# A new instruction order for the last two thirds of a fused adaLN, dilated-attention and SwiGLU block

## The chip, the cores and the metric

One core of a Trainium2 chip runs the whole program in one launch. The metric is the device time of one execution in microseconds; a kernel's time is the median of its runs. The profile is one execution recorded by the hardware profiler: its span runs from the first to the last recorded instruction, and its own time is a little longer than the span.

## The reference

A transformer block over 2048 tokens of width 512. A conditioning vector gives six vectors of 512 (shift, scale and gate for each half). The first half is a windowed attention: 32 heads of 16, each token looks at 8 keys, at distances 0, 2, ..., 14. The second half is a SwiGLU feed-forward network (FFN) with 1792 hidden units.

```python
mod = (_silu(c) @ w_mod).reshape(c.shape[0], 6, 1, -1)
sa, ca, ga, sb, cb, gb = ...
h = _layernorm(x) * (1 + ca) + sa
x = x + ga * _A_ref(h, A_wqkv, A_wo)      # window of 8, dilation 2
h = _layernorm(x) * (1 + cb) + sb
x = x + gb * _B_ref(h, B_w1, B_w3, B_w2)  # (silu(h w1) * (h w3)) w2
```

All inputs and the result are bfloat16.

## The kernel before

**How the work is cut.** The tokens are 16 tiles of 128. Attention runs by pairs of tiles; the last four are softmaxed as two pairs with one exponential step. The FFN runs in six blocks of tiles (list `FFN`): block 0 has tiles 0 and 1, block 1 tiles 2 and 3, block 2 tiles 4 to 7, block 3 tiles 8 to 11, block 4 tiles 12 and 13, block 5 tiles 14 and 15. Blocks 2 and 3 so have 512 columns, the others 256. Attention of late tiles runs beside the FFN of early ones.

**The steps of an attention tile T**, with the lines that the profile names:
- L742, VectorE: the product of queries and shifted keys ("product"), 4096 elements a partition.
- L752, TensorE: the scores, 16 small tiled matmuls, written S in the lists below.
- L764, L769 on VectorE: maximum and subtraction; L782 on ScalarE: the exponential, with a table load before it, and another (L889) when the next gate activation follows; L794, L796, L797 on VectorE: sum, reciprocal, normalisation; L807 on TensorE: a turn of the weights (T), copied out by L811 on ScalarE.
- The shifted values are loaded from a scratch tensor in device memory by four DMAs a tile (tiles `sb_vsh`, `sb_vshx`; three buffers in all). L827, VectorE: values times weights ("value product"). L855, TensorE: the sum over the window, 8 tiled matmuls ("value sum", A). L861 on ScalarE copies it to `sb_ac`; a DMA transposes it into `sb_ot`.
- L867, TensorE: the output projection (O), 4 matmuls. L871, VectorE: the residual, which also gives the sum for the mean.

**The second layer norm**, by pairs of tiles: L586 on GpSimd (minus the mean), L590 on ScalarE for each tile (squares and their sum), L596, L597, L599 on GpSimd (variance, power, bias), L601 on ScalarE for each tile (the normalised tile), a DMA transpose for each tile into `sb_h`, and L621 on ScalarE, four times for a block (scale and shift).

**The FFN.** For each of 14 hidden tiles of a block: the gate half (g, L883 with `w1`, 4 matmuls), L889 on ScalarE (silu), the up half (u, L883 with `w3`), L892 on VectorE (product of both). The second layer Z of a tile is 14 matmuls in two halves a and b of 7 (L921); for tiles 14 and 15 it is cut by columns instead, 28 matmuls of 256 columns each (L909). L931 on VectorE adds the residual, and a DMA stores the tile. L952 on VectorE scales `w2` by the gate vector, in four pieces.

**What sets the order.** `_build` records 1118 operations with what they read and write. The list `ORDER` says in which order they are issued, one list for all five engines, so each engine's own order is a part of it; `SLOTS` says which buffer each pooled value gets (8 banks of PSUM, 3 buffers for h, 5 for the normalised tiles, 6 for the silu results, 20 for the hidden tiles and so on). `synchronize` then derives the waits from data dependencies and from the reuse of buffers:

```python
for v in o.vals:
    if v.pool is not None and v.pool.last.get(v.slot) is not v:
        before = v.pool.last.get(v.slot)
        if before is not None:
            o.prev.extend(before.users)
```

Each engine executes its list strictly in that order, and a wait holds everything behind it on that engine. All but one of the DMAs are issued by SyncE (SP), in its own order, and a DMA's issue waits for its source and its target buffer.

Of the kernel before, what the change touches and what calls it, by code (L numbers as in the profile page):

```python
# [272 lines left out]
def _build(p, A_x, A_wqkv, A_wo, B_w1, B_w3, B_w2, c, w_mod, out):  # L273
# [752 lines left out]
]  # L1026
SLOTS = [
# [19 lines left out]
]  # L1047


# [26 lines left out]
```

## Time and profile before

| | us |
|---|---|
| median of 3 runs | 241.81 (240.87 to 242.73) |
| the profiled execution, its own time | 241.33 |
| its span | 239.6 |
| TensorE busy | 231.9 |
| VectorE busy | 179.2 |
| ScalarE busy | 138.8 |
| GpSimd busy | 30.0 |
| mean granted TensorE clock | 1.00 |

A row of the order in time has the start, the length, the engine, the line, the operation, the tiles (output first), and in brackets how long the engine sat idle before it and what released it. "PE" is TensorE's matmuls, "PEld" its weight loads, "SPq" the issuing of DMAs on SyncE. Rows merge equal neighbours, with their number behind an x.

### The profile page before, as it was taken

Reading aid. Unit: us, or ns where it says so; the run is one execution under the profiler, and the core shown is the slowest. Engines: PE = TensorE matmul, PEld = TensorE weight load, DVE = VectorE, ACT = ScalarE, POOL = GpSimd, SP = SyncE. Lnnn points to the kernel's source line nnn. Section 1 sums busy time; section 2 is a strip of 40 time slices with the busy share of each in tenths; the row PEclk is TensorE's granted clock in tenths of the full one; section 3 lists DMA queues with packets and bytes.
Section 4 is the critical chain, followed back from the end, with each engine's and each line's share of the span. In section 5 each row is a group of like instructions: output and inputs, shape, how many; then the busy total and the mean of one; then the engine's idle time right before and its main releaser. Section 6 shows DMA issues by size and latency. Waiting matters only on the chain.

```text
span 239.6 us, 4572 instructions
## 1 busy us (share of the span) xinstructions
PE 231.9 (97%) x1806; PEld 135.9 (57%) x1806; DVE 179.2 (75%) x279; ACT 138.8 (58%) x267; POOL 30.0 (13%) x66
## 2 busy tenths in 40 slices
PE   7899999999999999999999999988999999999995
PEld 4676554545688684664444444433374484566774
DVE  5689999999999999999999989381555125234243
ACT  2289577899978737958735792636466043322210
POOL 4434000013002000420005220032020000000000
PEclk9999999999999999999999999999999999999999
DMA  6999999999999995998953995341300700010102
GB/s 210 373 336 309 138 244 299 214 270 310 335 291 255 250 204 168 248 191 240 228 153 90 198 228 58 96 122 36 77 22 12 100 0 0 3 43 2 47 22 66
DMA packets 46317, 38.85 MB, mean 162 GB/s; under 512 B 21704, under 2 KB 37080, under 8 KB 46296
## 3 DMA queue, kind: packets, MB, share of 16 engines
q1 hardware_dynamic: 46288, 38.56, 67.7%
q8 instruction: 14, 0.23, 0.4%
q14 instruction: 7, 0.06, 0.1%
q10 hardware_dynamic: 8, 0.00, 0.0%
HBM read 29.62 MB, written 4.21 MB: 141 GB/s over the span
## 4 chain that ended last, share of the span: by engine, by line
PE 79%; DMA 6%; DVE 5%; SPq 4%; ACT 2%; POOL 2%; issue 1%; DVEq 0%
PE pall L883 36%; PE pall L921 16%; PE pall L691 7%; PE pall L867 6%; DMA sb_x<-in_A_x_dram 5%; SPq L124 4%; PE pall L711 4%; PE pall L752 3%; PE pall L855 3%; PE pall L909 3%; DVE sb_pq L742 2%; DMA sb_ot<-sb_ac 1%; DVE sb_vsh L827 1%; POOL sb_nm L586 1%; DVE sb_st L555 1%
## 5 line engine op out<-in xcount | busy, mean ns | idle before, releaser
L883 PE MATMUL pall<-sb_h,sb_w 128*128 128x256 bf16 (+1 forms) x672 | 102.9, 308 | 1.7 <-ACT sb_sg L889 1.7
L883 PEld LDWEIGHTS pall<-sb_h,sb_w 128*128 128x128 bf16 x672 | 64.8, 98 | 38.1 <-ACT sb_sg L889 2.1
L892 DVE TENSOR_TENSOR sb_hh<-sb_sg,pall 128x256 bf16<-128x256 bf16 (+1 forms) x84 | 40.0, 506 | 37.8 <-PE pall L883 32.6
L889 ACT ACTIVATE sb_sg<-pall 128x256 bf16<-128x256 f32 (+1 forms) x84 | 35.7, 453 | 50.9 <-PE pall L883 49.0
L921 PE MATMUL pall<-sb_w,sb_hh 128*128 128x512 bf16 x196 | 45.1, 379 | 0.0
L742 DVE TENSOR_TENSOR sb_pq<-sb_q,sb_kT 128x4096 bf16<-128x4096 bf16 x16 | 36.4, 2283 | 0.0
L691 PE MATMUL pall<-sb_h,sb_wqkv 128*128 128x512 bf16 (+1 forms) x160 | 31.1, 336 | 0.4 <-DVE sb_st L555 0.4
L921 PEld LDWEIGHTS pall<-sb_w,sb_hh 128*128 128x128 bf16 x196 | 19.1, 98 | 21.2 <-issue 0.4
L827 DVE TENSOR_TENSOR sb_vsh<-sb_vsh,sb_al 128x4096 bf16<-128x4096 bf16 x12 | 27.3, 2285 | 0.0
L621 ACT ACTIVATE sb_h<-sb_h,sb_modc 128x512 bf16<-128x512 bf16 (+1 forms) x24 | 16.5, 742 | 9.5 <-DMA sb_h<-sb_xn 9.5
L691 PEld LDWEIGHTS pall<-sb_h,sb_wqkv 128*128 128x128 bf16 x160 | 14.6, 97 | 12.1 <-DVE sb_st L555 0.6
L931 DVE TENSOR_TENSOR sb_o<-pall,sb_x 128x512 bf16<-128x512 f32 (+1 forms) x18 | 11.1, 625 | 10.0 <-PE pall L921 6.2
L586 POOL TENSOR_SCALAR sb_nm<-sb_sx 128x2 f32<-128x2 f32 x8 | 3.7, 464 | 108.4 <-DVE sb_x L871 108.3
L867 PE MATMUL pall<-sb_wo,sb_ot 128*128 128x512 bf16 x64 | 15.8, 379 | 0.5 <-DMA sb_ot<-sb_ac 0.5
L711 PE MATMUL pall<-sb_wqkv,sb_h 128*128 128x512 bf16 x64 | 16.0, 379 | 0.0
L871 DVE SCALAR_TENSOR_TENSOR sb_x<-pall,sb_x 128x512 bf16<-128x512 f32 x16 | 10.9, 687 | 4.6 <-PE pall L867 4.2
L644 ACT ACTIVATE sb_h<-pall,sb_modc 128x256 bf16<-128x256 bf16 (+1 forms) x18 | 9.9, 611 | 7.5 <-DVE sb_modc L509 6.5
L590 ACT ACTIVATE sb_xn<-sb_x,sb_nm 128x512 bf16<-128x512 bf16 x16 | 11.4, 716 | 4.8 <-POOL sb_nm L586 4.8
L861 ACT ACTIVATE sb_ac<-pall 128x512 bf16<-128x512 f32 x16 | 9.4, 597 | 7.0 <-PE pall L855 6.8
L601 ACT ACTIVATE sb_xn<-sb_x,sb_nb,sb_rs 128x512 bf16<-128x512 bf16 x16 | 12.2, 804 | 1.5 <-POOL sb_nb L599 1.4
L555 DVE BATCH_NORM_STATS2 sb_st<-sb_x 128x6 f32<-128x512 bf16 x16 | 10.5, 680 | 1.4 <-DMA sb_x<-in_A_x_dram 1.4
L701 ACT ACTIVATE sb_kT<-pall 128x512 bf16<-128x512 f32 x16 | 9.6, 606 | 2.8 <-PE pall L691 2.7
(87 smaller groups left out, 206.7 us busy)
## 6 DMA issues: line engine op xcount, KB each, us to landing
sb_vsh<-v_scratch_dram SPq DMA_DIRECT2D x48, 256.0 KB, 5.4
sb_vshx<-v_scratch_dram SPq DMA_DIRECT2D x16, 256.0 KB, 5.1
sb_w<-in_B_w_dram SPq DMA_DIRECT2D x6, 512.0 KB, 7.2
sb_w<-in_B_w_dram SPq DMA_DIRECT2D x6, 384.0 KB, 4.1
v_scratch_dram<-sb_v SPq DMA_DIRECT2D x16, 128.0 KB, 6.0
out_dram<-sb_o SPq DMA_DIRECT2D x14, 128.0 KB, 1.8
sb_wqkv<-in_A_wqkv_dram SPq DMA_DIRECT2D x6, 256.0 KB, 6.5
sb_x<-in_A_x_dram SPq DMA_DIRECT2D x4, 256.0 KB, 6.5
```

The source lines that it names most:

```text
L555: o = p.op("dve", lambda e, T=T: e.bn_stats(st[:, T, :], x_sb[:, T, :]), 595, ("st", T), r=[vx[T]], w=[vs])
L601: p.op("act", lambda e, vn=vn, T=T: e.activation(vn.at[:], x_sb[:, T, :], ACT.Identity, bias=nb[:, T, :], scale=rs[:, NT + T, :]), c_act(5 ...
L621: return e.activation(vh.at[:, ft, 0:n * P], vh.at[:, ft, 0:n * P], ACT.Identity, bias=modc[:, 8 * which + ft:8 * which + ft + 1], scale=m ...
L691: ins = e.matmul(bank(vp)[:, j * n:(j + 1) * n], wqkv[:, t, col:col + P], vh.at[:, t, 0:n], start=(t == ORDER[0] and j == 0), stop=(t == O ...
L711: ins = e.matmul(bank(vp), vh.at[:, t, tt * P:(tt + 1) * P], wqkv[:, t, 2 * D:3 * D], start=(t == ORDER[0]), stop=(t == ORDER[-1]))
L742: return e.tensor_tensor(vp.at[:], in0, in1, ALU.mult)
L827: return e.tensor_tensor(v_w, v_w, a_w, ALU.mult)
L867: ins = e.matmul(bank(vy), vt.at[:, ft, :], wo[:, ft, :], start=(ft == 0), stop=(ft == KT - 1))
L883: ins = e.matmul(bank(vp)[:, 0:n], wt[:, t, fi * P:(fi + 1) * P], vh.at[:, t, 0:n], start=(t == 0), stop=(t == KT - 1))
L889: p.op("act", lambda e: e.activation(vt.at[:, 0:n], bank(vgp)[:, 0:n], ACT.Silu), c_act(n), k, r=[vgp], w=[vt], table="silu")
L892: p.op("dve", lambda e: e.tensor_tensor(vh_.at[:, 0:n], vt.at[:, 0:n], bank(vup)[:, 0:n], ALU.mult), c_dve(n), k, r=[vt, vup], w=[vh_])
L921: ins = e.matmul(bank(vz), vhh[fi].at[:, tt * P:(tt + 1) * P], w2[:, fi, :], start=(fi == 0), stop=(fi == NF - 1))
```

## The change

`ORDER` and `SLOTS` get new contents; no other line of the file differs. Of the 1118 entries of `ORDER` the first 560 stay; from there on all engines have the same operations in a new order (on TensorE from its 187th operation of 384, on VectorE from the 131st of 263, on ScalarE from the 119th of 241, on GpSimd from the 41st of 62, on SP from the 89th of 168). `SLOTS` changes from its 74th entry on: of the first 560 operations 143 use another PSUM bank, and ten of TensorE's have their waits moved; their order is the same.

```diff
@@ ORDER
-    429, 710, 711, 456, 457, 712, 713, 722, 723, 724, 727, 728, 729, 455, 732, 733, 440, 725, 430, 746, 698, 699, 459, 53, 702, 703,
-    480, 54, 470, 471, 472, 734, 735, 441, 442, 460, 461, 345, 346, 714, 431, 432, 738, 762, 462, 481, 497, 482, 473, 474, 483, 675,
...
+    429, 710, 711, 456, 457, 712, 713, 702, 703, 727, 718, 719, 720, 721, 746, 747, 748, 749, 738, 480, 739, 740, 741, 714, 324,
+    455, 459, 715, 716, 717, 698, 699, 700, 732, 733, 53, 701, 440, 441, 442, 481, 430, 470, 471, 482, 54, 483, 460, 461, 722, 431,
...
@@ SLOTS
-    2, 3, 6, 1, 5, 0, 7, 5, 7, 6, 2, 2, 1, 4, 0, 1, 3, 1, 2, 0, 4, 1, 4, 0, 7, 0, 1, 3, 6, 3, 0, 4, 2, 5, 1, 2, 1, 1, 0, 2, 4, 0, 6,
+    2, 3, 6, 1, 5, 0, 7, 5, 7, 6, 2, 2, 1, 4, 0, 1, 3, 1, 2, 0, 4, 1, 4, 0, 7, 5, 1, 3, 6, 3, 0, 4, 2, 0, 1, 2, 1, 1, 0, 2, 4, 0, 1,
...
```

What the numbers mean, for TensorE from the last common operations to the first of block 4. g1.3 is the gate half of hidden tile 3 in block 1; S, A, O, T are scores, value sum, output projection and turn of a tile, Z4a the first half of tile 4's second layer. Before:

```
g1.3 u1.3 | g1.6 u1.6 u1.7 u1.8 g1.12 g1.0 g1.1 A7 g1.9 O5 A6 g1.4 O4 g1.10 O7 Z0b O6 u1.1 u1.4 u1.0 g1.5 u1.5 Z1b g1.13 u1.9 u1.12 T8 u1.10 u1.13 Z2a Z3a Z3b Z2b A9 S11 S10 A8
g2.3 g2.8 g2.11 u2.11 u2.8 g2.9 g2.7 O9 T10 O8 g2.12 g2.5 g2.0 u2.12 g2.2 g2.13 u2.5 A11 S12 S13 A10 g2.1 u2.2 u2.0 g2.6 g2.4 u2.1 S14 S15 O11 O10 u2.4 u2.6 u2.9 u2.3 g2.10 u2.7 u2.13 T12 u2.10 Z6a Z7a Z4a Z4b A13 A12 Z5a Z6b T14
g3.3 g3.1 O13 O12 g3.5 u3.5 g3.12 g3.4 u3.4 Z5b A15 A14 g3.9 u3.12 Z7b u3.1 g3.2 O14 O15 g4.4 ...
```

After:

```
g1.3 u1.3 | g1.1 g1.5 u1.5 g1.12 u1.12 g1.10 u1.10 g1.4 u1.4 g1.0 u1.0 u1.8 O5 A7 A6 g1.6 O4 g1.9 u1.9 u1.1 u1.7 T8 O7 O6 u1.6 Z1b Z0b g1.13 u1.13 Z2a Z2b Z3a Z3b S11 S10 A9 A8
g2.0 g2.2 u2.0 g2.12 g2.4 g2.10 u2.4 T10 O9 O8 g2.3 u2.3 g2.7 g2.5 g2.1 u2.1 u2.2 g2.11 A11 S13 S12 A10 g2.13 u2.10 u2.5 g2.8 u2.8 O11 g2.6 u2.6 S14 S15 g2.9 O10 u2.7 u2.11 u2.13 u2.12 u2.9 T12 Z5a Z7a Z6a Z6b Z7b A12 A13
g3.2 u3.2 T14 g3.0 Z4a g3.8 O12 u3.0 O13 g3.6 g3.9 Z4b g3.5 u3.5 g3.1 u3.8 A14 A15 g3.3 g3.12 u3.3 u3.6 g3.4 u3.4 Z5b g4.5 ...
```

Behind that, blocks 3 and 4 and the second layer of tiles 8 to 11 are mixed, then block 5 and the second layer of 12 to 15, in both orders; O14 and O15 come after 9 and 19 operations of that mixture in the new one.

On the other engines, as far as the text below speaks of them:
- VectorE, after value product 6: before, the residuals of 5, 4, 7 and 6 among two pieces of `w2`'s scaling (between 5 and 4) and the first sum of Z; after, residual 5, three softmax steps of tiles 8 and 9 around residual 4, both pieces of the scaling, residuals 7 and 6, one L892, the product for tile 11, three L892, the product for tile 10, value products 9 and 8, then four sums of Z mixed with L764 and L769 of tiles 10 and 11 (before: two sums there).
- VectorE around the end of attention: before, residuals 13 and 12 directly followed by value products 15 and 14; after, value product 15, residual 12, a sum of Z, an L892, residual 13, a sum of Z, value product 14.
- ScalarE: before, the L590 of tiles 13 and 12 stand ahead of the silu of three gate halves of block 3 that had been computed; after, they stand behind the silu of five.
- SP: before, all loads of the values of tile 9 are issued ahead of the transposes for tiles 4 to 7; after, its fourth load stands behind the first of these transposes. The write of tile 13's values to the scratch tensor goes ahead by some 25 us, the transposes of the value sums 5 and 4 stand between the two loads of `w2`.

78 rows, old and new, of tables (ORDER, SLOTS) are left out of this document.

## The prediction

> **What bounds the kernel now.** I read the page first, then the busy time by stretches of 10 us, then the chain that ended last, then TensorE (PE) alone in order of time, and last all engines around its gaps.
>
> ```profile
> span 239.6 us, 4572 instructions
> PE 231.9 (97%) x1806; PEld 135.9 (57%) x1806; DVE 179.2 (75%) x279; ACT 138.8 (58%) x267; POOL 30.0 (13%) x66
> ```
>
> ```profile
> 120.00:130.00 10.00, 10.00 (x87) 4.65 (x86) 10.00 (x11) 5.49 (x12) 2.07 (x2) 1.00 0.45 114
> ```
>
> PE is busy in 97% of the span (a stretch's first number is its length, the next PE, then weight loads, VectorE, ScalarE, GpSimd). Between 30 and 143 us VectorE (DVE) is as full as PE; this row is one of that stretch. So no order can win much: it can only close gaps on PE. A PE row's length holds its pipeline; what one operation occupies is read from the chain, where pieces follow without a gap.
>
> ```profile
> 118.17 0.86 PE pall L867 x4
> 119.04 0.22 PE pall L807 x4
> 120.12 6.04 PE pall L883 x28
> ...
> 225.96 2.62 PE pall L883 x24
> 228.58 1.51 PE pall L921 x7
> ...
> 230.97 6.13 PE pall L909 x56
> ```
>
> A wide matmul thus takes 0.216 us (6.04/28), so an FFN half of 4 (gate or up) 0.86 at 512 columns; 2.62/24 = 0.109, so 0.44 at 256 columns; half a second-layer tile 1.51; an output projection 0.86; a turn of the softmax 0.22. Now PE's starts, and what stands between them:
>
> ```profile
> 110.10 0.61 PE L855 MATMUL pall<-sb_vshx,sb_ind 128*32 128x512 bf16 x8
> ...
> 111.42 0.61 PE L855 MATMUL pall<-sb_vsh,sb_ind 128*32 128x512 bf16 x8
> 111.96 6.22 PE L883 MATMUL pall<-sb_h,sb_w 128*128 128x512 bf16 x28
> ...
> 149.24 1.05 PE L855 MATMUL pall<-sb_vsh,sb_ind 128*32 128x512 bf16 x16
> 150.22 3.19 PE L921 MATMUL pall<-sb_w,sb_hh 128*128 128x512 bf16 x14
> ```
>
> ```profile
> 156.93 3.62 PE L883 MATMUL pall<-sb_h,sb_w 128*128 128x512 bf16 x16
> ...
> 157.75 2.29 DVE L827 TENSOR_TENSOR sb_vshx<-sb_vshx,sb_al 128x4096 bf16<-128x4096 bf16 x1
> 157.92 2.19 POOL L586 TENSOR_SCALAR sb_nm<-sb_sx 128x2 f32<-128x2 f32 x1 [16.87 <-DVE sb_x L871]
> ...
> 160.14 0.72 ACT L590 ACTIVATE sb_xn<-sb_x,sb_nm 128x512 bf16<-128x512 bf16 x1 [4.14 <-POOL sb_nm L586]
> ...
> 161.57 1.06 ACT L889 ACTIVATE sb_sg<-pall 128x512 bf16<-128x512 f32 x2
> ...
> 162.20 1.04 PE L883 MATMUL pall<-sb_h,sb_w 128*128 128x512 bf16 x4 [1.66 <-ACT sb_sg L889]
> ...
> 166.16 1.90 PE L883 MATMUL pall<-sb_h,sb_w 128*128 128x512 bf16 x8
> ...
> 169.41 1.89 PE L883 MATMUL pall<-sb_h,sb_w 128*128 128x512 bf16 x8
> ...
> 171.81 1.90 PE L867 MATMUL pall<-sb_wo,sb_ot 128*128 128x512 bf16 x8 [0.51 <-DMA sb_ot<-sb_ac]
> ```
>
> Three gaps. (a) The 16 matmuls of 156.93 end at 160.39, the next start at 162.20: 1.81. (b) From 162.20 come 4 + 7 matmuls and the value sums of tiles 15 and 14 (0.98 for two, 149.24 to 150.22): 165.56, but the next start is 166.16: 0.60. (c) 169.41 + 1.73 = 171.14, next 171.81: 0.67, for the transposed value sum. Together 3.08 us, all in the stretch in which FFN block 3 runs beside the last attention tiles. From 112 to 153 PE has none, and from 173.5 to the last matmul (230.97 + 6.13) there is 0.2.
>
> Why (a): row 157.92 is the mean of tiles 12 and 13 on GpSimd (POOL). It begins 0.17 after a value product on DVE and takes 2.19 where the same operation takes 0.22 (row 95.83 below): it comes out 0.07 after the product. Behind it on ScalarE (ACT) stand two L590, and behind those the gate activation (161.57) that frees the bank PE wants.
>
> **The change, part by part.** Everything up to PE's 86.95 us (86.08 and two halves of 0.44) keeps its order; some PSUM banks there are renumbered, which moves ten PE waits to a neighbour. I count nothing for it. The last stage, from the first matmul of 230.97 to the end (239.6 - 230.97 = 8.63), has the same instructions and the same kind of tail, so also nothing. Three legs are left, in each of which I add PE's work in the new order and ask which chain is later.
>
> ```profile
> 94.90 0.58 ACT L782 ACTIVATE pall<-pall 128x512 f32<-128x512 f32 x1
> 95.50 1.28 ACT L889 ACT_TABLE_LOAD   x1
> 95.83 0.22 POOL L586 TENSOR_SCALAR sb_nm<-sb_sx 128x2 f32<-128x2 f32 x1 [18.51 <-DVE sb_x L871]
> 97.07 0.71 ACT L590 ACTIVATE sb_xn<-sb_x,sb_nm 128x512 bf16<-128x512 bf16 x1
> ...
> 98.66 0.19 POOL L596 TENSOR_SCALAR sb_rs<-sb_var 128x2 f32<-128x2 f32 x1 [2.62 <-ACT sb_xn L590]
> 99.10 0.70 POOL L597 TENSOR_TENSOR sb_rs<-sb_rs,sb_cst 128x2 f32<-128x2 f32 x1
> 99.88 0.19 POOL L599 TENSOR_TENSOR sb_nb<-sb_nm,sb_rs 128x2 f32<-128x2 f32 x1
> 99.94 2.28 DVE L742 TENSOR_TENSOR sb_pq<-sb_q,sb_kT 128x4096 bf16<-128x4096 bf16 x1
> ...
> 101.13 1.51 ACT L601 ACTIVATE sb_xn<-sb_x,sb_nb,sb_rs 128x512 bf16<-128x512 bf16 x2
> 101.96 5.15 SPq L124 DMA_TRANSPOSE sb_h<-sb_xn  x4
> 103.29 0.60 ACT L811 ACTIVATE sb_al<-pall 128x512 bf16<-128x512 bf16 x1 [0.38 <-PE pall L807]
> 106.27 0.41 DVE L892 TENSOR_TENSOR sb_hh<-sb_sg,pall 128x256 bf16<-128x256 bf16 x1
> 106.60 2.29 DVE L827 TENSOR_TENSOR sb_vshx<-sb_vshx,sb_al 128x4096 bf16<-128x4096 bf16 x1
> 108.62 2.93 ACT L621 ACTIVATE sb_h<-sb_h,sb_modc 128x512 bf16<-128x512 bf16 x4 [3.33 <-DMA sb_h<-sb_xn]
> 111.64 0.69 DVE L764 TENSOR_REDUCE sb_mx<-pall 128x64 f32<-128x512 f32 x1
> 111.95 0.11 PEld L883 LDWEIGHTS pall<-sb_h,sb_w 128*128 128x128 bf16 x2 [0.42 <-ACT sb_h L621]
> ```
>
> *Leg 1, to the first half of block 2 (111.96 before).* Up to there PE has 20 halves of 0.44 (8.7), 4 projections (3.4), 2 value sums together (1.1), a turn (0.2), 6 second-layer halves (9.1) and two scores with two value sums (111.96 - 110.10 = 1.9): 24.4, ready at 111.35, against 111.96. But row 111.95 shows that PE waited there for L621, the last link of the layer norm of tiles 4 to 7, and this is what counts. The chain begins with projection 6, the last of the four. In the new order PE reaches it at 86.95 + 11.3 = 98.3, its end (99.15) and DVE's residuals of 7 and 6 (behind the two w2 scalings) put residual 6 at 99.68. POOL starts 0.78 after a residual starts (95.05 to 95.83 in the row's stage): 100.46. ACT is busy with L601 of tile 4 and a gate until 101.3, then two L590 of 0.71; 0.88 after the second starts (98.66 stands so to the L590 behind 97.07) L596, then L597 and L599 (98.66 to 100.07), done near 104.1. Two L601 (1.51) end at 105.6; two transposes at 1.25 on SP (row 101.96: four in 5.15) end at 107.5, against 107.11. L621 begins 1.5 after that (108.62 - 107.11) and PE 3.34 after L621 begins: 112.35. That is 0.4 later than before, though PE would have been 0.6 earlier.
>
> *Leg 2, to the first half of block 3.* PE: 28 wide halves 24.2, scores and value sums 1.9 + 1.0 + 1.0, 4 projections 3.4, 2 turns 0.4, now 5 second-layer halves ahead of it, 7.6: 39.4, ready at 151.8. The chain: the scores of tiles 14 and 15 come after 22 halves, 3 projections, a turn and 1.9, and take 0.9, so at 136.95; DVE's L764 and L769 (0.69 each as 111.64) 138.3; two exponentials (0.58 each), the table (1.28) and gate 9 (0.5) on ACT 141.2; two L590, POOL's three, L601, L811, L601 as above (1.5 + 1.25 + 2.1) 146.1; one transpose 147.35; to PE 1.5 + 3.34 again: 152.2. DVE must deliver value product 12 by 150.8: its operations there are those of before with one more of 0.6, and its span then, 111.00 to 149.5, holds 0.6 idle, so it ends near 149.9. That cover of 0.9 is the narrowest in this leg.
>
> *Leg 3, to 230.97 before.* Here the new order has 17 of block 3's halves ahead of block 4 where the old one had 11, and projections 14 and 15 go behind block 4's first halves: 17 x 0.86 + 2 projections 1.7 + 3 second-layer halves 4.5 + 1.0 + 0.2 = 22.1. On ACT the means of tiles 12 and 13 now stand behind the gates that PE needs first; on DVE no product follows residual 13 until value product 14, after second-layer tile 4. So (a) has no cause: while POOL and ACT work on the mean, PE has five halves (4.3) at hand. (b) goes as the two sums now run together after eleven halves; (c) goes as projection 14 now starts some 11 us after its value sum; in the old order it came 6 us after (165.5 to 171.81). The layer norm of 12 and 13 is due at 174.3, and I have its L621 end near 173. Then block 4, the other 11 halves of block 3, 8 + 4 second-layer halves, 2 projections, block 5: 12.2 + 9.5 + 18.1 + 1.7 + 12.2 = 53.8, and the 0.2 of before. Each bank passes from PE over ACT to PE with at least one half between, as it does now without a gap. 152.2 + 22.1 + 53.8 + 0.2 = 228.3.
>
> Sum: 228.3 - 230.97 = -2.7 us: +0.4 of leg 1, some +0.2 of leg 2 and -3.1 for (a) to (c), less two switches between tiled and full matmuls (0.1 each: 111.42 to 111.96 is 0.54 where 110.10 to 110.54 is 0.44). The profiled execution took 241.33, 1.73 more than its span; 241.33 - 2.7 = 238.6. It lies 0.48 under the median of the three runs (241.81), so 239.1 on that scale. With (a) to (c) closed and nothing given back it would be 241.33 - 3.3 = 238.0.
>
> **The rivals.** *First: POOL is shut out in leg 1.* POOL's L586 for tiles 6 and 7 would start at 100.46, and DVE's product for tile 11 at 100.63 (residual 0.62, then one L892 of 0.33 as 106.27 to 106.60). Row 99.88 is for me: POOL 0.06 ahead of a product ran its normal 0.19. Row 157.92 is against: 0.17 behind one cost 2 us. If POOL falls behind, the mean comes out at 102.95, ACT's gate 13 and the norm follow, and block 2 starts 1.9 later, all else shifting: 241.0. The Trainium skill (SBUF — State Buffer, "SBUF: two separate sides") says that VectorE and GpSimd take their shared port pair as an exclusive lock for a whole instruction, whoever starts first. By that rule a margin of any size decides wholly, so 239.1 or 241.0; the two rows agree with it.
>
> *Second: DVE slips in leg 2.* Full for 38 us, it now takes four second-layer sums among the first softmax steps of tiles 10 and 11, where it had two. Each wait adds to its end; before it had one, of 0.6. Three such waits would use the cover of 0.9 and open 1 to 2 us on PE: 240.1 to 241.5.
>
> *Third, the slow side: the last quarter of tile 9's values.* Before, all four of its loads are issued ahead of the norm's transposes; now the fourth stands on SP behind the first transpose, which waits for L601 of tile 4, so it is issued at 102.3.
>
> ```profile
> DMA to landing us min/median/max: 3.2/4.9/11.2
> ```
>
> DVE wants it at 106.4. At 3.2 to 4.9 it costs 0 to 0.8; at 11.2 it lands at 113.5, 7.1 late, and as DVE has only 0.9 to give, PE stands for 6.2: 239.1 + 6.2 = 245.3. It is slower than 241.81 from 7.7 us of landing on. For it speaks that transposes share the queue; against it that the loads around it are few just then.
>
> *Fourth: the renumbered banks change the first third.* The waits move by one or two PE operations; within 0.2 either way.
>
> **How the numbers follow.** Forecast 0.52, 238.0 to 240.0; first rival 0.17; second 0.17; third 0.14, about two thirds of it beyond +1%. The prediction is 239.1. For 8 in 10 the range takes the forecast from its floor, and the first two rivals; a slight case of the third goes in up to the highest run of before, so 237.9 to 242.7. About 1% (2.4 us) is what a measurement tells from no change: 239.4 and 244.2. Faster: most of the forecast, 0.46; slower 0.11; the rest, 0.43.
>
> **What would show it.** Right: in the changed profile no PE gap over 0.3 between the first half of block 3 and the first L909; the first half of block 2 at 112.3 and still released by L621; POOL's L586 of tiles 6 and 7 at 0.22. Wrong: that operation at 2 us (first rival); value sum 12 released by DVE and late (second); value product 9 released by a DMA (third); a new gap in front of a projection or of block 4's first half in leg 3, which would undo the forecast's main term.

## The result and the profile after

The changed kernel takes 241.11 us (median of 22 runs, 239.53 to 245.11), the kernel before 242.06 (22 runs, 240.87 to 242.93). The ratio is 0.9943, 95% interval 0.992 to 0.9966: faster by 0.6%, where 1.1% was forecast (239.1 against 241.81). The ratios of this text leave out executions that took over 1.5% more than the fastest of their kernel. The profiled execution of the changed kernel took 241.63. It is the longest of the 13 of the 22 that ran at a mean granted clock of 0.999 or 1, whose median is 240.01, so it is one of the slower draws and not a typical one.

The page of that execution, its first two lines that answer to those of before:

```profile
span 239.9 us, 4563 instructions
PE 232.0 (97%) x1806; PEld 137.0 (57%) x1806; DVE 179.5 (75%) x279; ACT 139.5 (58%) x267; POOL 29.9 (12%) x66
```

PE's work and share are what they were, and this execution's span is 0.3 us longer. PE in order of time (start, length, and in brackets the idle time before a piece with what ended it):

```profile
86.08 3.67 PE L883 MATMUL pall<-sb_h,sb_w 128*128 128x256 bf16 x32
90.20 2.79 PE L883 MATMUL pall<-sb_h,sb_w 128*128 128x256 bf16 x24 [0.45 <-DVE sb_hh L892]
...
93.96 1.05 PE L855 MATMUL pall<-sb_vsh,sb_ind 128*32 128x512 bf16 x16
...
98.03 0.38 PE L807 MATMUL pall<-sb_ident,sb_attn 128*128 128x128 bf16 x4
101.05 1.90 PE L867 MATMUL pall<-sb_wo,sb_ot 128*128 128x512 bf16 x8 [2.63 <-DMA sb_ot<-sb_ac]
...
115.11 6.22 PE L883 MATMUL pall<-sb_h,sb_w 128*128 128x512 bf16 x28
...
154.88 1.90 PE L883 MATMUL pall<-sb_h,sb_w 128*128 128x512 bf16 x8
...
230.94 6.28 PE L909 MATMUL pall<-sb_w,sb_hh 128*128 128x256 bf16 x56
```

The reader is to see three things. The first third is as before: 86.08 stands in both. Leg 1 ends at 115.11, 3.15 later than before (111.96), with a wait of 2.63 at 101.05 and a small one of 0.45 at 90.20. Leg 2 is 154.88 - 115.11 = 39.77 and leg 3 230.94 - 154.88 = 76.06, together 115.83 where before needed 230.80 - 111.96 = 118.84 (by the same view), and no row of theirs has an idle time in it: gaps (a), (b) and (c) are gone. The tail from L909 on is 8.96 (239.9 - 230.94) against 8.80. Sum: +3.15 - 3.01 + 0.16 = +0.30, the difference of the two spans.

So in this execution the gain came as a whole and was given back in leg 1. The chain of waits shows to what:

```profile
94.03 0.57 PE pall L855 x8
...
95.12 0.13 ACT sb_ac L861
95.25 5.75 DMA sb_ot<-sb_ac
```

The value sum of tile 7 ends at 94.6, ScalarE copies it, SP issues its transpose at 95.25, and that is 5.75 us under way before projection 7 can start. From the end of that value sum to the wait PE has 3.8 us of other work (to 98.4). Before, it was 3.9: value sum 7 was done at 90.7 and projection 7 started at 94.62, without a wait, for the transpose, issued at 91.40, landed in 2.3. So it is not the cover that shrank. What changed is what SP issues ahead of the transpose: three loads of tile 9's values at 89.75 and one of tile 8's at 94.62, 256 KB each, where the old order issues the first of them behind the transposes, at 94.85. SP's rows, and PE's for projection 7, before:

```profile
91.40 3.40 SPq L124 DMA_TRANSPOSE sb_ot<-sb_ac  x2
94.62 1.03 PE L867 MATMUL pall<-sb_wo,sb_ot 128*128 128x512 bf16 x4
94.85 1.87 SPq L124 DMA_DIRECT2D sb_vshx<-v_scratch_dram  x3
```

SP's rows after:

```profile
89.75 2.31 SPq L124 DMA_DIRECT2D sb_vshx<-v_scratch_dram  x3
94.62 0.51 SPq L124 DMA_DIRECT2D sb_vsh<-v_scratch_dram  x1
95.25 3.09 SPq L124 DMA_TRANSPOSE sb_ot<-sb_ac  x2
```

Two statements on the lists above are inexact. `SLOTS` differs from its 69th entry on. And of the three silus behind L590 of tiles 13 and 12 in ScalarE's old order only those of g3.5 and g3.12 follow directly; that of g3.4 stands behind L601.

### The profile page after: what moved, and what is told of

Same layout as the page of the kernel before. It is cut to its first block, busy times and chain, and to the rows that moved or that the text cites. A ratio compares the mean times of both kernels' runs of the same rounds, so it can differ in the third digit from the quotient of the medians.

```text
span 239.9 us, 4563 instructions
## 1 busy us (share of the span) xinstructions
PE 232.0 (97%) x1806; PEld 137.0 (57%) x1806; DVE 179.5 (75%) x279; ACT 139.5 (58%) x267; POOL 29.9 (12%) x66
## 4 chain that ended last, share of the span: by engine, by line
PE 82%; DMA 8%; ACT 3%; DVE 3%; SPq 1%; issue 1%; ACTq 0%; DVEq 0%
PE pall L883 39%; PE pall L921 18%; PE pall L691 6%; PE pall L867 5%; DMA sb_vsh<-v_scratch_dram 3%; PE pall L711 3%; PE pall L909 3%; DMA sb_ot<-sb_ac 2%; DVE sb_vsh L827 2%; PE pall L855 2%; PE pall L752 2%; DMA sb_h<-sb_xn 2%; PE pall L518 2%; SPq L124 1%; PE pall L636 1%; ACT sb_h L621 1%
## 5 line engine op out<-in xcount | busy, mean ns | idle before, releaser
L892 DVE TENSOR_TENSOR sb_hh<-sb_sg,pall 128x256 bf16<-128x256 bf16 (+1 forms) x84 | 39.9, 505 | 31.5 <-PE pall L883 26.5
L921 PE MATMUL pall<-sb_w,sb_hh 128*128 128x512 bf16 x196 | 44.6, 379 | 0.0
L827 DVE TENSOR_TENSOR sb_vsh<-sb_vsh,sb_al 128x4096 bf16<-128x4096 bf16 x12 | 27.3, 2287 | 1.6 <-DMA sb_vsh<-v_scratch_dram 1.5
L621 ACT ACTIVATE sb_h<-sb_h,sb_modc 128x512 bf16<-128x512 bf16 (+1 forms) x24 | 16.1, 741 | 6.6 <-DMA sb_h<-sb_xn 6.6
L586 POOL TENSOR_SCALAR sb_nm<-sb_sx 128x2 f32<-128x2 f32 x8 | 3.7, 465 | 121.7 <-DVE sb_x L871 121.7
L601 ACT ACTIVATE sb_xn<-sb_x,sb_nb,sb_rs 128x512 bf16<-128x512 bf16 x16 | 12.3, 806 | 7.0 <-POOL sb_nb L599 6.8
L590 ACT ACTIVATE sb_xn<-sb_x,sb_nm 128x512 bf16<-128x512 bf16 x16 | 11.4, 713 | 3.7 <-POOL sb_nm L586 3.7
L867 PEld LDWEIGHTS pall<-sb_wo,sb_ot 128*128 128x128 bf16 x64 | 6.1, 98 | 9.1 <-DMA sb_ot<-sb_ac 3.1
L721 ACT ACTIVATE sb_v<-pall 128x512 bf16<-128x512 f32 x16 | 9.5, 600 | 2.8 <-PE pall L711 2.8
```

Source lines behind the costliest of these rows:

```text
L590: p.op("act", lambda e, vn=vn, T=T: e.activation(vn.at[:], x_sb[:, T, :], ACT.Square, bias=nm[:, T, :], accum_out=var[:, T, :]), c_act(512 ...
L601: p.op("act", lambda e, vn=vn, T=T: e.activation(vn.at[:], x_sb[:, T, :], ACT.Identity, bias=nb[:, T, :], scale=rs[:, NT + T, :]), c_act(5 ...
L621: return e.activation(vh.at[:, ft, 0:n * P], vh.at[:, ft, 0:n * P], ACT.Identity, bias=modc[:, 8 * which + ft:8 * which + ft + 1], scale=m ...
L827: return e.tensor_tensor(v_w, v_w, a_w, ALU.mult)
L867: ins = e.matmul(bank(vy), vt.at[:, ft, :], wo[:, ft, :], start=(ft == 0), stop=(ft == KT - 1))
L892: p.op("dve", lambda e: e.tensor_tensor(vh_.at[:, 0:n], vt.at[:, 0:n], bank(vup)[:, 0:n], ALU.mult), c_dve(n), k, r=[vt, vup], w=[vh_])
```

## The experiments

Theory Q (queue): the later legs keep their whole gain; leg 1 is lost because the transposes of value sums 7 and 6 stand behind value loads in the DMA queue. Its rivals were that the transfers are late by chance, whatever stands ahead (theory J, jitter), that the bytes and not their order are at fault, that the three gaps had other causes, and that the later legs are short only because leg 1 did work for them. What follows uses these measurements; each profile is of one execution.

| kernel | median us (runs) | ratio to before, 95% | PE's wait at projection 7 or 6 | block 2 starts | L909 starts | span |
|---|---|---|---|---|---|---|
| changed, first group | 241.11 (22) | 0.9943, 0.992 to 0.9966 | 2.63 | 115.11 | 230.94 | 239.9 |
| changed, second | 239.87 (9) | 0.9907, 0.9874 to 0.994 | 2.17 | 113.70 | 229.53 | 238.5 |
| changed, third | 240.58 (6) | 0.9879, 0.9812 to 0.9946 | 0.41 | 111.93 | 227.76 | 236.7 |
| loads behind | 239.84 (12) | 0.9904, 0.9871 to 0.9938 | 0.34 | 113.36 | 229.19 | 238.1 |
| store late | 240.21 (12) | 0.9941, 0.9903 to 0.9979 | 1.77 | 112.98 | 228.81 | 237.7 |
| loads refitted | 239.81 (12) | 0.9917, 0.9883 to 0.995 | 0.78 | 114.44 | 230.26 | 239.2 |
| first leg undone | 239.29 (6) | 0.9885, 0.9854 to 0.9916 | none | 112.61 | 228.44 | 237.4 |
| first leg undone, again | 239.74 (6) | 0.989, 0.9827 to 0.9952 | none | 115.20 | 231.03 | 240.0 |
| first leg alone | 248.93 (6) | 1.0272, 1.0228 to 1.0316 | 2.33 | 118.17 | 239.02 | 247.8 |
| before, loads ahead | 246.77 (6) | 1.0141, 1.0075 to 1.0207 | 3.52 | 119.09 | 237.91 | 246.7 |
| before, gap (a) alone | 242.85 (12) | 1.0034, 1.0005 to 1.0063 | none | 112.64 | 231.94 | 240.7 |

In the diffs the numbers are entries of `ORDER`: 497 to 500 are the loads of tile 9's values, 487 to 490 of tile 8's, 472 and 462 the transposes of value sums 7 and 6, 778 to 781 those of the layer norm of tiles 4 to 7, 324 the store of tile 13's values. Only SP's entries are shown where only SP's order is changed.

**The changed kernel once more.** No edit; expected:

> The changed kernel once more, beside the others on the same chip. Theory Q (queue): projection 7 waits in many executions for the transposed value sum 7, because four quarter loads of values and a piece of w2 are issued ahead of that transpose; so its times fall into two groups, near 239.7 and near 241.7, median 240 to 242. Theory J (jitter): the transfers of this stretch are late by chance, whatever stands ahead; same times, and none of the other kernels of this call differs from it.

PE's row of the wait and the start of block 2:

```profile
99.64 1.90 PE L867 MATMUL pall<-sb_wo,sb_ot 128*128 128x512 bf16 x8 [2.17 <-DMA sb_ot<-sb_ac]
...
113.70 6.22 PE L883 MATMUL pall<-sb_h,sb_w 128*128 128x512 bf16 x28
```

The wait is at the same place, 2.17 long, and block 2 to L909 is 115.83 again. The ratio's interval and that of the first group overlap (0.992 to 0.994). The two groups of times that were expected did not come: all nine executions lie between 239.37 and 240.66.

**The loads of tiles 9 and 8 behind the transposes.**

```diff
-  ... 497, 499, 500, 487, 472, 462, 488, 490, 489, 778, 498, 779 ...
+  ... 472, 462, 497, 499, 500, 487, 488, 490, 489, 778, 498, 779 ...
```

> The changed kernel with four quarter loads (three of tile 9, one of tile 8) issued behind the transposes of value sums 7 and 6 instead of ahead of them. Theory Q: the transposes land 2.3 to 3.5 us after issue instead of 5.1 to 5.8, the gap of 2.6 us before projection 7 goes, median 239.0 to 239.8 and no group near 241.7. Theory J: 241, as the changed kernel. A third outcome: value product 9 then waits for its loads, up to 1 us, 240.5.

```profile
98.34 1.04 PE L867 MATMUL pall<-sb_wo,sb_ot 128*128 128x512 bf16 x4 [0.34 <-DMA sb_ot<-sb_ac]
...
112.67 0.61 PE L855 MATMUL pall<-sb_vsh,sb_ind 128*32 128x512 bf16 x8 [1.49 <-DVE sb_vsh L827]
```

Issued ahead of the loads, the transposes landed 2.3 and 3.1 us after their issue, and the wait shrank from 2.17 to 0.34 (now at projection 6). That is what theory Q says of the place. The profile of the unedited kernel above is the one to compare with, as in both the value loads issued between 80.4 and 82.0 us landed after a median of 5.8 us; the two transposes took a median of 2.7 here and 4.8 there. But a second wait stands at 112.67, for DVE's value product (L827): the last load of tile 9, behind the first norm transpose as before and with seven other loads now pushed up against it, was issued at 102.36 and took 5.7 us. The ratio, 0.9904, is that of the unedited kernel. So this order didn't pay: the wait moved to the transfer that was pushed back.

**The store of tile 13's values later.**

```diff
-  ... 324, 455, 53, 440, 430 ... 781, 330 ...
+  ... 455, 53, 440, 430 ... 781, 324, 330 ...
```

> The changed kernel with the store of tile 13's values (128 KB) put back to where it stood before, behind the transposes of the normalised tiles 4 to 7. Theory Q: the queue is 0.5 us shorter from 83 us on; the loads of tiles 7 and 6 and all transposes behind land 0.5 earlier, median 0.3 to 0.7 below the changed kernel. Theory J: no difference.

With 128 KB less in the queue the wait was 1.77 and block 2 started at 112.98, but the ratio, 0.9941, is not below that of the unedited kernel on the same chip (0.9907). Inconclusive: by the last experiment below the wait differs by more than this between executions of one kernel.

**Before, with the loads ahead of the transposes.** The reverse, in the old order.

```diff
-  ... 54, 472, 462, 497, 498, 499, 487, 490 ...
+  ... 54, 497, 498, 499, 487, 472, 462, 490 ...
```

> The kernel before with the same four quarter loads issued ahead of the transposes of value sums 7 and 6, as the changed kernel has them; nothing else is moved. Theory Q: projection 7 (94.62 in the profile of before) gets its input only near 97 to 98, and the norm of tiles 4 to 7 follows: 243.5 to 245, 2 us over the kernel before. Theory J: 242.0, as before.

```profile
100.08 1.15 PE L867 MATMUL pall<-sb_wo,sb_ot 128*128 128x512 bf16 x4 [3.52 <-DMA sb_ot<-sb_ac]
...
169.33 1.04 PE L883 MATMUL pall<-sb_h,sb_w 128*128 128x512 bf16 x4 [1.65 <-ACT sb_sg L889]
```

The old order gets the same wait, 3.52, at the same line, and gap (a) is still there at 169.33. 1.4% slower: four loads ahead of two transposes make this wait without anything else of the new order. In four of its six executions, the profiled one among them, the clock fell as well (mean 0.993), so its span holds more than the wait. The two at full clock took 244.39 and 244.50, 2.1 and 2.2 us over the median of before (242.30), which is what theory Q expected and theory J did not.

**Before, with gap (a) taken away alone.** ScalarE's two L590 of tiles 13 and 12 (956, 955) and the GpSimd step behind them (957) go behind the silus of g3.5 and g3.12 (931 the last).

```diff
-  954, 956, 955, 583, 957, 902, 904, 903, 930, 931, 898,
+  954, 583, 902, 904, 903, 930, 931, 956, 955, 957, 898,
```

> Before, with ACT's two variance instructions of tiles 13 and 12 (L590), and the POOL step that reads them, moved behind the next two silus; nothing else changed. Theory (the gap of 1.81 at 160.39 is ACT queued behind POOL's step of tile 13): this gap goes, L909 begins 1.4 to 1.8 us earlier (229.2 to 229.6), the gaps of 0.60 and 0.67 behind it stay, ratio to before 0.992 to 0.995. Rival (PE would have waited there for DVE's value product all the same): the gap shrinks by less than 0.5, or one of that size stands behind it, ratio 0.998 to 1.002.

GpSimd, then ScalarE, then PE in order of time:

```profile
158.64 2.19 POOL L586 TENSOR_SCALAR sb_nm<-sb_sx 128x2 f32<-128x2 f32 x1 [16.91 <-DVE sb_x L871]
```

```profile
164.10 1.52 ACT L601 ACTIVATE sb_xn<-sb_x,sb_nb,sb_rs 128x512 bf16<-128x512 bf16 x2 [1.66 <-POOL sb_nb L599]
165.53 0.57 ACT L889 ACTIVATE sb_sg<-pall 128x512 bf16<-128x512 f32 x1
```

```profile
166.24 0.62 PE L855 MATMUL pall<-sb_vsh,sb_ind 128*32 128x512 bf16 x8 [2.06 <-ACT sb_sg L889]
```

Gap (a) is gone from its place (PE runs from 157.65 to 163.57 and on without a wait), but the rival's outcome came, a wait of that size behind it, though not from DVE's value product, which the rival named: GpSimd's L586 still took 2.19, the rest of the norm came out late, and ScalarE stood 1.66 for it at the next step of the same chain, L601, with the next silu (165.53, of g3.4) behind. PE waited 2.06 there instead. That is the place of gap (b), where before the same silu ended a wait of 0.23. The ratio, 1.0034, misses the theory's 0.992 to 0.995 and lies just above the rival's 0.998 to 1.002; four of the twelve executions had a mean clock of 0.993. So the prediction's cause of (a) is right as to the chain, and the order of one step doesn't close it.

**The loads refitted in the changed kernel.**

```diff
-  ... 497, 499, 500, 487, 472, 462, 488, 490, 489, 778, 498, 779 ...
+  ... 497, 499, 500, 472, 462, 498, 487, 488, 490, 489, 778, 779 ...
```

> The changed kernel with one of tile 8's value loads moved behind the transposes of value sums 7 and 6, and the last load of tile 9 moved ahead of the other three of tile 8 and of the first norm transpose; the first three of tile 9 stay ahead, where the queue otherwise stands empty. Theory (it is the order in the queue that made the wait): value sum 7 lands 2.3 to 3.5 us after its issue, the wait at projection 7 is 0 to 0.8, none before the value products of tiles 9 and 8, block 2 starts at 111.6 to 112.6, span 236.3 to 237.4, ratio 0.984 to 0.988. Rival (the bytes set it, not their order: some transfer is late whichever goes last): the wait comes back at the value products or at the norm transposes, block 2 at 113.2 or later, ratio 0.990 or above, as with the loads moved behind.

```profile
99.33 1.04 PE L867 MATMUL pall<-sb_wo,sb_ot 128*128 128x512 bf16 x4 [0.78 <-DMA sb_ot<-sb_ac]
...
114.44 6.22 PE L883 MATMUL pall<-sb_h,sb_w 128*128 128x512 bf16 x28 [1.84 <-ACT sb_h L621]
```

The wait at the projection shrank to 0.78, none was left at the value products, and 1.84 came up in front of block 2, for L621: the norm transposes are what is late now. The chain names the last of them:

```profile
107.11 4.32 DMA sb_h<-sb_xn
...
111.45 2.94 ACT sb_h L621 x4
```

The rival's numbers came (block 2 at 113.2 or later, ratio 0.9917), but they don't show its cause. This transpose took 4.32 us where the same one took 2.4 in each profile of the changed kernel. At 2.4 it would have landed at 109.5, 1.9 earlier, which is the whole wait. The 16 DMA engines were far from full then (busy share 0.51 from 108 to 110 us, 0.21 from 110 to 112), so neither the bytes nor the order of the loads explains it; why it was slow stays open. This execution took 240.92, 1.1 over the kernel's median.

**The first leg undone: the old order up to block 2, the new one behind it.**

```diff
+ cut = 680   # the first gate matmul of block 2 in the old order
+ ORDER = OLD[:cut] + [n for n in NEW if n not in OLD[:cut]]
```

Buffers are those of the old list for what begins before the cut and of the new list behind it; three values got another free one.

> The order of before up to the first matmul of the first layer of block 2, the order of after from there on. At this cut PE has issued the same matmuls in both orders; only two transposed or loaded values and a few copies lie on the other side. Theory (what was lost lies in the first leg alone, and legs 2 and 3 keep their gain without it): block 2 starts at 111.8 to 112.3, leg 2 takes 39.7 to 40.0, leg 3 76.0 to 76.2, so L909 begins at 227.6 to 228.5, the span is 236.4 to 237.5 and the ratio to before 0.986 to 0.990, below the 0.9907 of the changed kernel. Rival (the later legs are short because the first one ran the value loads of tiles 10 and 12 and two copies ahead of the cut): leg 2 takes 41 or more, and the ratio is 0.991 or above.

```profile
112.61 6.22 PE L883 MATMUL pall<-sb_h,sb_w 128*128 128x512 bf16 x28
...
152.38 1.90 PE L883 MATMUL pall<-sb_h,sb_w 128*128 128x512 bf16 x8
...
228.44 6.28 PE L909 MATMUL pall<-sb_w,sb_hh 128*128 128x256 bf16 x56
```

```profile
sb_vsh<-v_scratch_dram SPq DMA_DIRECT2D x3, 256.0 KB, 7.1
```

Leg 2 is 152.38 - 112.61 = 39.77 and leg 3 76.06, to the digit those of the changed kernel; block 2 starts 0.3 later than the theory's upper end. The span, 237.4, and the ratio, 0.9885, are within what was expected. The rival on the later legs falls. The last row says that the value loads issued between 80.4 and 82.1 us took a median of 7.1 us to land, almost as long as in the first profile of the changed kernel (7.6, below), and yet no projection waited: the old first leg stands a slow queue.

**The first leg alone: the new order up to block 2, the old one behind it.** As above with the lists exchanged.

> The order of after up to the first matmul of block 2, the order of before from there on. Theory (the first leg of the changed order is a loss by itself): a wait of 2 to 2.7 us at the projection of tile 7 for the transposed value sum, block 2 starts at 113.5 to 115.2, the legs behind it keep the 119.0 of before with the gap of about 1.8 at the first of block 3's value work, L909 begins at 232.5 to 234.2, ratio to before 1.006 to 1.013. Rival (the first leg pays for work that shortens the later ones): the later legs fall below 117.5, ratio 0.999 or below.

```profile
100.60 3.07 PE L867 MATMUL pall<-sb_wo,sb_ot 128*128 128x512 bf16 x8 [2.33 <-DMA sb_ot<-sb_ac]
...
118.17 6.22 PE L883 MATMUL pall<-sb_h,sb_w 128*128 128x512 bf16 x28 [1.67 <-DVE sb_o L931]
126.17 1.04 PE L867 MATMUL pall<-sb_wo,sb_ot 128*128 128x512 bf16 x4 [1.78 <-DMA sb_ot<-sb_ac]
```

```profile
102.00:104.00 2.00, 2.00 (x7) 0.87 (x6) 0.82 (x3) 0.04 (x1) 0.00 (x0) 0.50 1.10 228
```

A loss, as the theory has it, but of 2.7% where 0.6 to 1.3% was expected. The wait at projection 7 is there (2.33). What was not in that estimate: the granted clock (the third number from the end of the last row) is 0.50 behind that wait, so the eight projection matmuls took 3.07 instead of 1.90; and the splice itself has two waits that neither kernel has, 1.67 at 118.17 and 1.78 at 126.17. The size can't be put down to leg 1 for that reason.

**The changed kernel and the first leg undone, on one chip.** No edit.

> The changed kernel once more, on the same chip as the run with its first leg undone. Theory (the one wait of 2.2 to 2.7 us at projection 7 also lets the granted clock fall in part of the executions): some executions show a mean clock of 0.993, and these are 1.5 to 3 us longer than the others; those at full clock lie at 239.5 to 240.8. Rival (the low clock falls on every kernel alike): as many of the executions of before, and of the kernel with the first leg undone, show it.

> The order of before up to block 2 and that of after from there on, again, beside the changed kernel on one chip. Theory (PE has no wait over 0.5 us left, so neither the wait nor the clock costs): median 238.8 to 239.5, at most one execution at a clock of 0.993, and 0.5 to 1.5 us below the changed kernel's median. Rival (the earlier result was the chip's): median as the changed kernel's or above.

The changed kernel's profile, PE in order of time:

```profile
97.61 2.16 PE L867 MATMUL pall<-sb_wo,sb_ot 128*128 128x512 bf16 x8 [0.41 <-DMA sb_ot<-sb_ac]
...
111.93 6.22 PE L883 MATMUL pall<-sb_h,sb_w 128*128 128x512 bf16 x28
...
151.70 1.90 PE L883 MATMUL pall<-sb_h,sb_w 128*128 128x512 bf16 x8
...
227.76 6.28 PE L909 MATMUL pall<-sb_w,sb_hh 128*128 128x256 bf16 x56
```

Here the wait is 0.41, and this execution took 238.41 us; the prediction has 238.6 on the profile's scale and 112.3 for block 2. The legs behind it are 39.77 and 76.06 once more. The same kernel, in three profiles: wait 0.41, 2.17, 2.63; block 2 at 111.93, 113.70, 115.11; time 238.41, 240.18, 241.63. SP issued the transpose of value sum 7 at 94.06, 94.34 and 95.25, so the issue explains a little. The rest is how long transfers took. The DMA view, median us from issue to landing: for each of the three profiles in this order, the value loads issued between 80.4 and 82.1 us, then the transposes of value sums 7 and 6:

```profile
sb_vsh<-v_scratch_dram SPq DMA_DIRECT2D x3, 256.0 KB, 4.2
sb_ot<-sb_ac SPq DMA_TRANSPOSE x2, 3.0
```

```profile
sb_vsh<-v_scratch_dram SPq DMA_DIRECT2D x3, 256.0 KB, 5.8
sb_ot<-sb_ac SPq DMA_TRANSPOSE x2, 4.8
```

```profile
sb_vsh<-v_scratch_dram SPq DMA_DIRECT2D x3, 256.0 KB, 7.6
sb_ot<-sb_ac SPq DMA_TRANSPOSE x2, 5.4
```

4.2, 5.8 and 7.6 us for the loads, and 3.0, 4.8 and 5.4 for the transposes behind: the wait at projection 7 grows with what the queue still has to do when leg 1 begins, and this backlog is brought along: the value loads issued from 60 to 70 us, ahead of any change, took 6.4, 7.1 and 7.6 in the same three profiles. By the Trainium skill (DMA: Bandwidth & Descriptors, "Queues, rings and completion order") the DMAs that SP issues share one row of rings, and in each ring descriptors are consumed in order. By that rule a short transfer has to sit out most of what was issued ahead of it, and these rows agree. So both theories have a part: chance sets how long the queue is, and the order sets whether PE stands for it.

The rest of the expectations fared worse. Two of the six executions of the changed kernel had a mean clock of 0.993 or less (242.34 and 242.60), but three of the six with the first leg undone had it too, and three of eleven of before: the theory that the wait at projection 7 makes the low clock is not borne out here. In the profiled execution with the first leg undone the busy time by stretches puts the low clock (third number from the end) far ahead of any changed instruction:

```profile
8.00:12.00 4.00, 3.10 (x48) 2.40 (x49) 2.54 (x10) 1.01 (x2) 0.37 (x2) 0.87 1.08 373
12.00:16.00 4.00, 4.00 (x30) 2.94 (x29) 2.54 (x7) 1.10 (x3) 0.72 (x2) 0.70 1.11 350
```

Its block 2 therefore starts at 115.20, and the 115.83 behind it are the same. The median of 239.74 is above the 238.8 to 239.5 expected. It and the changed kernel's 240.58 differ in the expected direction, but six runs each that overlap (238.92 to 242.16 and 238.41 to 242.60) don't show one faster than the other. The first leg undone beats before in both groups (0.9885 and 0.989); that it beats the changed kernel is not shown.

## Why the prediction was right and wrong

- *The three gaps (a) to (c) as the only thing to win, and that all three close*: right. Leg 3 was forecast at 22.1 + 53.8 + 0.2 = 76.1 and measured 76.06, leg 2 at 39.85 and measured 39.77, and the two together at 115.82 or 115.83 in all eight profiles that have the new order there, whatever came ahead. In leg 2 the fit is in part luck: the forecast ended it with L621's chain, and what was measured is PE's own work, which the forecast put at 39.4 (its terms give 39.5).
- *What closes them*: the kernel with (a) alone bears out the chain from GpSimd's L586 over ScalarE to PE, and shows that it is a chain with several links; which move of the new order closes (a) is not tested, and of (b) and (c) it is only shown that they went.
- *Leg 1, "In the new order PE reaches it at 86.95 + 11.3 = 98.3"* (projection 6): this is the step that failed. It counts PE's work up to the projections and takes it that their inputs are there; of what SP issues, only the last load of tile 9 was weighed, and not the other loads that move ahead of the transposes of value sums 7 and 6. With the 2.3 us that such a transpose took before, projection 7 could have started at 95.25 + 2.3 = 97.55 in the first profile, ahead of PE; it took 5.75. The term is the sum of leg 1, put at +0.4 and measured, by the start of block 2, at -0.03, +1.74 and +3.15 (the leg had begun 0.39, 0.11 and 0 earlier than before).
- *Which link ends leg 1*: the prediction let L621 release block 2, before as after, because of its row 111.95. That is a misreading. The row is one of weight loads, and its 0.42 also stands in front of the weight loads at 110.10, without a releaser, and again in the first profile after, where L621 ended at 114.80 and block 2 began at 115.11:

```profile
110.10 0.12 PEld L855 LDWEIGHTS pall<-sb_vshx,sb_ind 128*32 128x32 bf16 x8 [0.42 <-issue]
...
111.95 2.06 PEld L883 LDWEIGHTS pall<-sb_h,sb_w 128*128 128x128 bf16 x11 [0.42 <-ACT sb_h L621]
```

```profile
115.11 5.73 PEld L883 LDWEIGHTS pall<-sb_h,sb_w 128*128 128x128 bf16 x28 [0.42 <-ACT sb_h L621]
```

  PE's own rows have no idle time there, in the profile before and the three of the changed kernel. Behind the wait at projection 7 comes PE's work alone: from there to block 2 it is 14.06 in the first two profiles of the changed kernel (115.11 - 101.05 and 113.70 - 99.64). So the +0.4 was worked out from a chain that did not decide, and PE's sum of 24.4 was short: before took 111.96 - 86.95 = 25.0, with 0.19 of waiting. Only with the loads refitted did L621 end last: block 2 began 0.06 after it, against 0.41 before and 0.31 in the first profile after.
- *First rival, GpSimd shut out in leg 1*: did not happen; L586 of tiles 6 and 7 took 0.22, as this row of the changed kernel's GpSimd shows.

```profile
103.78 0.22 POOL L586 TENSOR_SCALAR sb_nm<-sb_sx 128x2 f32<-128x2 f32 x1 [2.72 <-DVE sb_x L871]
```

- *Second rival, DVE slips in leg 2*: no wait for DVE there.
- *Third rival, the last load of tile 9 late behind a transpose*: the right resource and the wrong transfer. Loads held up transposes, not the other way round. Where the loads were moved behind, its own wait did come up, with 1.49 and not the 6.2 that its worst case was priced at.
- *Fourth rival, other banks*: nothing seen; 86.08 in both profiles, and 85.97 and 85.69 in the other two of the changed kernel.
- *The tail at nothing*: 0.16 longer.
- *The sum*: 228.3 is added up from starts of the order in time, but 230.97 is the start of L909 in the chain view, which puts it 0.17 later than the order in time (230.80). So the legs as forecast give -2.5, not -2.7.
- *The clock, at nothing*: the changed kernel's 22 runs fall into 13 at a mean clock of 0.999 or 1 (239.53 to 241.63, median 240.01) and nine at 0.993 or less (241.46 to 245.11); the prediction has no term for that. The clock of before's 22 is not on record, but none took more than 242.93, and in the later groups six of 60 executions of before had a clock that low and took 244.07 or more. Of the changed kernel's 37 in all groups eleven had it. With the loads ahead of the transposes it is 23 of 61 executions (changed, store late, before with loads ahead, first leg alone), in the other kernels 14 of 108 (among them loads refitted, where three of the four loads are still ahead, with none of 12). That leans towards a part of the waits in leg 1, but doesn't show it: the three low executions that were profiled had the low clock behind a wait at a projection (two) and at 8 to 16 us (one), and none of the changed kernel's own eleven was profiled.

Direction and range held, and the size did not: 0.95 between the medians where 2.7 was forecast. That the range held is luck, as it was wide for the sake of rivals that did not happen. Of the 1.75 that are missing, 0.65 are missing at full clock (240.01 against 242.06), where the loss in leg 1 differs from one execution to the next, from nothing to as much as the gain behind it. The other 1.1 go with the executions at the lower clock, and what lowers it stays open.

## What to carry to other kernels

When an order is costed by adding up one engine's work, write beside each operation the time at which its input can be there, and for a DMA take the landing time behind what the new order issues ahead of it, not that of a row in which the queue had run empty (here 2.3 us became 3.5 to 5.75 for the transpose of value sum 7). In a full queue the order decides who waits: put first what the bottleneck engine wants first, and see by experiment what is then last. One profile is one draw of such a queue; look at two or three before a wait is costed.

## What was not expected of the hardware

The time from issue to landing of the same loads, in the same order and issued within a microsecond of one another, differed between executions of one kernel by almost a factor of two (medians of 4.2 to 7.6 us).

Behind a wait on TensorE the granted clock can stand at half, so that more is lost than the wait's length; that the wait is the reason is not shown, and one profile had 0.50 from 11 to 14 us, with waits of 0.85 and 0.34 ahead. Behind the wait of 2.33 the clock was 0.50 from 102 to 104 us, and so it was behind the 3.52 of the old order with the loads ahead; behind the 2.63 of the changed kernel it stayed at 1.00. The same stretch of these two:

```profile
102.00:104.00 2.00, 2.00 (x6) 0.63 (x5) 0.43 (x1) 0.00 (x0) 0.00 (x0) 0.50 1.06 236
```

```profile
102.00:104.00 2.00, 2.00 (x13) 1.10 (x12) 1.71 (x6) 0.18 (x1) 0.22 (x1) 1.00 1.05 231
```

The Trainium skill (TensorE: Matmul & The Clock Gate, "The HAM clock gate") gives half clock after at least one idle window of about 3.4 us, with windows that run freely. Half clock is what the rows show, and that its onset differs from one execution to the next fits windows that are not tied to the program; but no wait of 3.4 us stood ahead of the drop behind 2.33, so in this case the length that page states is not a bound below which a wait is safe.
